# Four 32-byte gaps in the tile pools of an attention and two-layer kernel

## The chip, the core and the metric

The kernel runs on one core of one Trainium2 chip. The metric is the device time of one execution in microseconds (us). The kernel before was timed in three runs: 2345.20, 2345.23 and 2346.77 us, median 2345.23.

## What is computed

```python
def _attn_ref(q, k, v, tau):                     # q, k, v: 2 x 6016 x 256, float32
    qn = q / (np.linalg.norm(q, axis=1, keepdims=True) + 1e-06)
    kn = k / (np.linalg.norm(k, axis=1, keepdims=True) + 1e-06)
    s = kn.transpose(0, 2, 1) @ qn / tau
    a = np.exp(s - s.max(-1, keepdims=True))
    a /= a.sum(-1, keepdims=True) + 1e-09
    return v @ a
x = attn_out.reshape(12032, 256)
h = x @ w_in                                     # w_in: 256 x 2048
x = (h - np.tanh(h)) @ w_out                     # w_out: 2048 x 256
gate = 1.0 / (1.0 + np.exp(-(x @ w_gate)))       # w_gate, w_val: 256 x 1536
out = (gate * (x @ w_val)) @ w_out2              # w_out2: 1536 x 256
```

## The kernel before

The 12032 tokens are cut into 24 blocks, 12 for each batch. A block is 500 tokens wide in 20 of the 24; blocks 6 and 18 are 512 wide and blocks 7 and 19 are 504 wide. A first stage (about the first 100 us) loads q and k of batch 0 and forms their 256 x 256 product, its softmax and the product of that matrix with w_in, so that each batch has its own input weights (tiles awh and awl, the "hi" and "lo" halves of a float32 split in two float32r numbers). For batch 1 the same is done in between, beside the blocks of batch 0.

From then on a block p is four families of matmuls, all of them 128 x 128 weights against a moving operand as wide as the block:

- H (lines 324 and 326): the weights awh and awl against vTh and vTl, 16 groups of 6 matmuls a block.
- X (lines 370, 371 and 373): the weights w1h and w1l against the split activations g, 16 groups of 6.
- GV (lines 405, 406 and 408): the weights wgh, wgl, wvh and wvl against x2h and x2l, 12 groups of 12.
- O (line 437): the weights w2h and w2l against the split products p, 12 groups of 6.

Two blocks run interleaved: a slot of the main loop has one group of H of block p, one of GV of block p-1, one of X of block p (two groups behind its H) and one of O of block p-1, in this order on TensorE; some slots have no GV, no O or neither, so that a block has 408 matmuls, 192 of them H and X. X and O are built alike: four matmuls on the hi half with hi and lo weights, then two on the lo half with hi weights, moving operands from the same pool "rr". The first block, and the first four groups of block 1, do X in plain float32 (line 365). The main loop is written out under a manual schedule, so the order on every engine is the program's, with no planner.

The tiles lie in pools, one pool after another in the order in which they are opened, and in a pool tag after tag in the order of first use. A tile takes its bytes per partition, rounded up to 32. Every big tile here is a multiple of 64 bytes, so what a tile's start is modulo 64 comes from the small tiles ahead of it. The program of the kernel before has these starts, in bytes in the partition:

| tiles | used as | start | modulo 64 | modulo 128 |
|---|---|---|---|---|
| pool const: ones, ident, 4 tiles of 4 bytes (32 each) | | 16512 | 0 | 0 |
| pool wp: awh, awl, w1h, w1l (2048 each) | weights of H and X | 17664 | 0 | 0 |
| pools wk, cv, rr, sx (2048 each) | moving: g, p; float32 X | 83200 | 0 | 0 |
| pool one: x2h, x2l, vTh, vTl (4096 each) | moving of GV and H | 134400 | 0 | 0 |
| pool one: rn, mx, sm (32 each), then aT, acc (2048 each) | aT, acc: moving of GV of block 0, weights of line 285 | 150880 | 32 | 96 |
| pool wp2: wgh, wgl, wvh, wvl, w2h, w2l (2048 each) | weights of GV and O | 154976 | 32 | 96 |

wp2 takes the place of the pools boot1, boot4, boot6 and boot3 of the first stage, which are opened at the same 154976 and closed before it. In them raw (q and k) is both weights and moving operand of line 562.

All slices within these tiles begin at a multiple of 512 bytes, so a slice is where its tile is, modulo 64 and modulo 128.

TensorE loads the weights of the next matmul (rows "PEld") beside the running one, so at any time two reads of the partition run: the moving operand of matmul i and the weights of matmul i+1.

Of the kernel before, what the change touches and what calls it, by code (L numbers as in the profile page):

```python
# [8 lines left out]
F32 = mybir.dt.float32  # L9
# [8 lines left out]
P = 128  # L18
# [8 lines left out]
def kernel(  # L27
# [46 lines left out]
    const = ctx.enter_context(tc.tile_pool(name="const", bufs=1))  # L74
    wp = ctx.enter_context(tc.tile_pool(name="wp", bufs=1))
# [6 lines left out]
    one_p = ctx.enter_context(tc.tile_pool(name="one", bufs=1))  # L82
# [14 lines left out]
    def psw(name, shape=(P, 512)):  # L97
        return ps_w.tile(list(shape), F32, tag="w", name=name)
# [15 lines left out]
    aw_lo = {}  # L114
    w1_hi = [wp.tile([P, 2, C], F32R, name=f"w1h{i}") for i in range(N1 // 2)]
    w1_lo = {}
    win_d = dr_p.tile([N1 // 2, P, NK, 2 * P], F32, name="win_d")

    def conv(src, shape, pool, tag, name, w=None, hi=None, lo=None):
# [78 lines left out]
    def norm_mm(b, sq, sk, first, last):  # L198

        for o, xs in ((0, sq), (2, sk)):  # L200
            for i, x in enumerate(xs):
                for ct in range(2):
                    MM(nrm[b][:, o + ct, :], x[:, ct * P:(ct + 1) * P], ones[:, :NW],
                       start=first and o + i + ct == 0, stop=last and i == len(xs) - 1, skip_group_check=True)

    def s_softmax(b, sq, sk):

        np_ = nrm.get(b)
        if np_ is None:
            np_ = nrm[b] = psw(f"n{b}", (P, 4, NW))  # L210
        norm_mm(b, sq, sk, b == 1, True)
        yield
        rn = one_p.tile([P, 4], F32, tag="rn", name=f"rn{b}")
        nc.scalar.activation(rn, np_[:, :, 0], AF.Sqrt)
        if b == 0:
            nc.scalar.activation(dummy, dummy, AF.Exp)
        yield
        nc.vector.tensor_scalar_add(rn, rn, 1e-6)
        nc.vector.reciprocal(rn, rn)

        dg = (cv if b else wk)(f"dg{b}", (P, 2, P))
        for ct in range(2):
            nc.vector.tensor_scalar(dg[:, ct, :], ident, rn[:, ct:ct + 1], None, ALU.mult)
        nc.vector.tensor_scalar(rn[:, 2:4], rn[:, 2:4], rtau[:, 0:1], None, ALU.mult)
        s = (cv if b else wk)(f"s{b}", (P, 2, C))
        if b:
            yield
        for ct in range(2):
            nc.scalar.activation(
                s[:, ct, :], (ks[b] if b else kq[b])[:, ct, :], AF.Copy, scale=rn[:, 2 + ct:3 + ct]  # L230
            )
        if b:
            yield
        rq = psw(f"rq{b}", (P, 2, P))
        for ct in range(2):
            MM(rq[:, ct, :], ones, dg[:, ct, :], start=ct == 0, stop=True, skip_group_check=True)
        yield
        mx = one_p.tile([P, 2], F32, tag="mx", name=f"mx{b}")
        for ct in range(2):
            nc.vector.tensor_tensor(  # L240
                out=s[:, ct, :], in0=s[:, ct, :], in1=rq.rearrange("p a c -> p (a c)"), op=ALU.mult
            )
            nc.vector.tensor_reduce(
                out=mx[:, ct:ct + 1], in_=s[:, ct, :], axis=AX.X, op=ALU.max, negate=True
            )
        yield
        sm = one_p.tile([P, 2], F32, tag="sm", name=f"sm{b}")
        for ct in range(2):
            nc.scalar.activation(
                s[:, ct, :], s[:, ct, :], AF.Exp, bias=mx[:, ct:ct + 1], accum_out=sm[:, ct:ct + 1]  # L250
            )
        yield
        for ct in range(2):
            sc = sm[:, ct:ct + 1]
            nc.vector.tensor_scalar_add(sc, sc, 1e-9)
            nc.vector.reciprocal(sc, sc)
            nc.vector.tensor_scalar(s[:, ct, :], s[:, ct, :], sc, None, ALU.mult)
        if b:
            yield
        else:  # L260
            aT[b] = one_p.tile([P, 2, C], F32, tag="aT", name=f"aT{b}")
        ep = psw(f"ep{b}", (P, 2, C)) if b else None
        for ct in range(2):
            cs = slice(ct * P, (ct + 1) * P)
            e = ep[:, :, cs] if b else psw(f"ep{b}_{ct}", (P, 2, P))
            for kk in range(2):
                nc.tensor.transpose(e[:, kk, :], s[:, ct, kk * P:(kk + 1) * P], ident)
            if b == 0:
                nc.scalar.activation(aT[b][:, :, cs], e, AF.Copy)
        yield  # L270
        if b:
            hi = one_p.tile([P, 2, C], F32R, tag="aT", name=f"aTh{b}")
            lo = one_p.tile([P, 2, C], F32R, tag="acc", name=f"aTl{b}")
            nc.scalar.activation(hi, ep, AF.Copy)
            nc.vector.tensor_tensor(out=lo, in0=ep, in1=hi.bitcast(F32), op=ALU.subtract)
            aT[b] = (hi, lo)
# [246 lines left out]
    cb_t = const.tile([P, 1], F32, name="cb")  # L523
    ct_t = const.tile([P, 1], F32, name="ct")
    dummy = const.tile([P, 1], F32, name="dummy")
    nc.vector.memset(cb_t, CB)
    nc.vector.memset(ct_t, -HT * HT)
    cb, ct2 = cb_t[:, 0:1], ct_t[:, 0:1]
# [3 lines left out]
    with tc.tile_pool(name="boot1", bufs=1) as boot1, tc.tile_pool(name="boot4", bufs=4) as boot4, \  # L532
# [99 lines left out]


        sm0 = s_softmax(0, *sq)
        tv = split_v(0)
        for step in (tail[0], tail[0], tail[0], tv, tail[1], tv, sm0, sm0, e_mm, e_mm, sm0, tail[1], e_mm, e_mm,
# [6 lines left out]
        next(w6)  # L643

    wp2 = ctx.enter_context(tc.tile_pool(name="wp2", bufs=1))
    wg_hi, wg_lo, wv_hi, wv_lo = (
        [wp2.tile([P, 2, 2 * P], F32R, name=f"{nm}{i}") for i in range(N2 // 2)]
        for nm in ("wgh", "wgl", "wvh", "wvl")
# [69 lines left out]
    for j in range(NT):  # L718
        t = 54 + 2 * j
        at(t - 2, s1_load, j)  # L720
        at(t, s1_square, j)
    ts = t + 1
    at(ts, lambda: s_softmax(1, [acc[1][:, 0, :]], [acc[1][:, 1, :]]))
    at(20, e_out)
    at(28, e_out)
# [115 lines left out]
```

## Time and profile before

| | |
|---|---|
| time, median of three runs | 2345.23 us |
| span of the profiled execution, first to last instruction | 2342.6 us |
| TensorE (PE) busy | 2330.5 us, 99% of the span |
| weight loads (PEld) busy | 1932.8 us, 83% |
| VectorE (DVE) busy | 1799.2 us, 77% |
| ScalarE (ACT) busy | 1575.5 us, 67% |
| GpSimd (POOL) busy | 67.2 us, 3% |
| matmuls | 10338 |

The profiled execution has only its span; the median of the runs is 2.6 us above it, for what lies around the first and the last instruction. Matmuls overlap in the trace (a duration of 386 ns, while the next starts after some 224 ns), so what a matmul costs is read from the distance of two starts, or from a stretch of time divided by the matmuls in it, and not from its duration.

### The profile page before, as it was taken

The numbers are of one execution on the slowest core, as the hardware profiler recorded it, in microseconds if no ns is written. First come the engines' busy times: TensorE is split into PE (matmuls) and PEld (weight loads), VectorE is DVE, ScalarE is ACT, GpSimd is POOL, SyncE is SP. The second block draws the span as 40 slices with busy tenths as digits, with TensorE's granted clock in tenths as the row PEclk, the third lists the DMA queues.
The fourth block names the chain that finished last, engine by engine and source line by source line (L and its number), as shares of the span: only waits on it lengthen the run. The fifth ranks groups of instructions, "written<-read, shape, count | busy, mean of one in ns | idle before, by whom it ended". The sixth has DMA issues, their size and how long they took to land.

```text
span 2342.6 us, 28855 instructions
## 1 busy us (share of the span) xinstructions
PE 2330.5 (99%) x10338; PEld 1932.8 (83%) x10338; DVE 1799.2 (77%) x2791; ACT 1575.5 (67%) x2777; POOL 67.2 (3%) x53
## 2 busy tenths in 40 slices
PE   9999999999999999999999999999999999999999
PEld 7778788888888888888888888888888888888887
DVE  7999877787878777777777777777777777777773
ACT  6677666776767667766676666666666666666663
POOL 0000000111111110000000000000000000000000
PEclk9999999999999999999999999999999999999999
DMA  9742001101101100000000000000000000000000
GB/s 353 225 132 90 27 1 50 33 26 50 32 28 45 32 27 18 1 23 32 18 18 14 6 18 1 18 18 1 18 18 1 18 18 1 18 1 18 10 1 18
DMA packets 54000, 86.54 MB, mean 37 GB/s; under 512 B 4960, under 2 KB 34144, under 8 KB 53856
## 3 DMA queue, kind: packets, MB, share of 16 engines
q1 hardware_dynamic: 53280, 83.91, 11.1%
q8 instruction: 81, 1.33, 0.2%
q10 hardware_dynamic: 576, 0.79, 0.1%
q14 instruction: 63, 0.52, 0.1%
HBM read 69.73 MB, written 14.94 MB: 36 GB/s over the span
## 4 chain that ended last, share of the span: by engine, by line
PE 90%; DVE 7%; ACT 1%; issue 1%; DMA 0%; ACTq 0%; DVEq 0%; SPq 0%
PE o L437 16%; PE h L324 14%; PE h L326 7%; PE x L373 7%; PE x L370 7%; PE x L371 7%; PE ga L405 5%; PE ga L406 5%; PE va L405 5%; PE va L406 5%; PE ga L408 5%; PE va L408 5%; DVE accb L573 1%; DVE w L341 1%; DVE w L342 1%
## 5 line engine op out<-in xcount | busy, mean ns | idle before, releaser
L339 DVE SCALAR_TENSOR_TENSOR w<-u,h 128x500 f32<-128x500 f32 (+2 forms) x384 | 259.3, 675 | 327.0 <-ACT t L335 326.8
L334 ACT ACTIVATE u<-h 128x500 f32<-128x500 f32 (+2 forms) x384 | 223.7, 583 | 248.0 <-PE h L326 245.5
L342 DVE COPY_PREDICATED w<-m,t 128x500 f32<-128x500 uint16 (+2 forms) x384 | 306.2, 797 | 39.9 <-ACT sr L679 0.5
L337 ACT ACTIVATE s<-u,cb 128x500 f32<-128x500 f32 (+2 forms) x384 | 274.5, 715 | 0.7 <-DVE w L341 0.6
L338 ACT ACTIVATE m<-u,ct 128x500 bf16<-128x500 f32 (+2 forms) x384 | 272.8, 710 | 0.0
L340 DVE TENSOR_TENSOR t<-h,t 128x500 f32<-128x500 f32 (+2 forms) x384 | 258.2, 672 | 0.0
L341 DVE SCALAR_TENSOR_TENSOR w<-s,w 128x500 f32<-128x500 f32 (+2 forms) x384 | 257.3, 670 | 0.0
L324 PE MATMUL h<-vTh,awh 128*128 128x500 f32 (+2 forms) x768 | 243.9, 399 | 0.0
L324 PE MATMUL h<-vTl,awh 128*128 128x500 f32 (+2 forms) x768 | 235.4, 387 | 0.9 <-DVE vTl L311 0.9
L326 PE MATMUL h<-vTh,awl 128*128 128x500 f32 (+2 forms) x768 | 235.5, 388 | 0.0
L335 ACT ACTIVATE t<-h 128x500 f32<-128x500 f32 (+2 forms) x384 | 223.6, 582 | 1.7 <-PE x L365 1.0
L405 PE MATMUL ga<-x2h,wgh 128*128 128x500 f32 (+2 forms) x552 | 213.6, 387 | 0.0
L406 PE MATMUL va<-x2h,wvl 128*128 128x500 f32 (+2 forms) x552 | 213.6, 387 | 0.0
L406 PE MATMUL ga<-x2h,wgl 128*128 128x500 f32 (+2 forms) x552 | 213.6, 387 | 0.0
L405 PE MATMUL va<-x2h,wvh 128*128 128x500 f32 (+2 forms) x552 | 213.4, 387 | 0.0
L417 DVE TENSOR_TENSOR sg<-va,sg 128x500 f32<-128x500 f32 (+2 forms) x288 | 192.3, 668 | 20.9 <-PE va L408 20.9
L416 ACT ACTIVATE sg<-ga 128x500 f32<-128x500 f32 (+2 forms) x288 | 169.2, 587 | 15.7 <-PE ga L408 12.8
L408 PE MATMUL ga<-x2l,wgh 128*128 128x500 f32 (+2 forms) x576 | 176.1, 387 | 0.0
L408 PE MATMUL va<-x2l,wvh 128*128 128x500 f32 (+2 forms) x576 | 176.0, 387 | 0.0
L324 PEld LDWEIGHTS h<-vTh,awh 128*128 128x128 f32 x768 | 143.6, 188 | 34.5 <-issue 7.1
L324 PEld LDWEIGHTS h<-vTl,awh 128*128 128x128 f32 x768 | 144.4, 188 | 30.6 <-DVE vTl L311 1.4
L326 PEld LDWEIGHTS h<-vTh,awl 128*128 128x128 f32 x768 | 144.2, 188 | 28.9
(361 smaller groups left out, 4449.8 us busy)
## 6 DMA issues: line engine op xcount, KB each, us to landing
v<-in_v_dram SPq DMA_DIRECT2D x20, 500.0 KB, 4.2
out_dram<-ob SPq DMA_DIRECT2D x19, 500.0 KB, 3.2
sr<-in_q_dram SPq DMA_DIRECT2D x47, 128.0 KB, 2.1
sr<-in_k_dram SPq DMA_DIRECT2D x47, 128.0 KB, 2.2
raw<-in_q_dram SPq DMA_DIRECT2D x13, 384.0 KB, 8.1
raw<-in_k_dram SPq DMA_DIRECT2D x12, 384.0 KB, 8.2
st_wi<-in_moe_w_in_dram SPq DMA_DIRECT2D x8, 512.0 KB, 7.0
st_w<-in_moe_w_out_dram SPq DMA_DIRECT2D x8, 512.0 KB, 4.8
```

What stands on the lines that cost most here:

```text
L324: MM(o[:, :n], aw_hi[i][:, kk, fs], x[:, kk, :n], start=x is h and kk == 0, stop=False)
L326: MM(o[:, :n], aw_lo[i][:, kk, fs], h[:, kk, :n], start=False, stop=kk == 1)
L337: nc.scalar.activation(s, u, AF.Square, bias=cb)
L338: nc.scalar.activation(m, u, AF.Relu, bias=ct2)
L339: nc.vector.scalar_tensor_tensor(out=w, in0=u, scalar=C2, in1=hp, op0=ALU.mult, op1=ALU.mult)
L340: nc.vector.tensor_tensor(out=t, in0=hp, in1=t, op=ALU.subtract)
L341: nc.vector.scalar_tensor_tensor(out=w, in0=s, scalar=CG, in1=w, op0=ALU.add, op1=ALU.mult)
L342: nc.vector.copy_predicated(w, m.bitcast(U16), t)
L405: MM(o[:, :n], wht[m // 2][:, d, ms], h[d][:, :n], start=d == 0, stop=False)
L406: MM(o[:, :n], wlt[m // 2][:, d, ms], h[d][:, :n], start=False, stop=False)
L408: MM(o[:, :n], wht[m // 2][:, d, ms], lo[d][:, :n], start=False, stop=d == 1)
L437: MM(ops[p][d][:, :n], w[i][:, a, ds[d]], x, start=m == 0 and w is w2_hi and x is ph, stop=m == N2 - 1 and x is pl)
```

## The change

Four tiles of 8 float32 (32 bytes in the partition) are added that nothing writes or reads. One stands at the end of const, ahead of wp; one at the end of wp, ahead of wk; one in the pool one, between sm and aT; one at the start of wp2. No instruction is added or moved. Added up, const's gap moves wp by 32 bytes, with wp's gap everything from wk to vTl moves by 64, aT, acc and the pools of the first stage by 96, and the tiles of wp2 by 128.

```diff
@@ -114,6 +114,7 @@
     w1_hi = [wp.tile([P, 2, C], F32R, name=f"w1h{i}") for i in range(N1 // 2)]
     w1_lo = {}
+    wp.tile([P, 8], F32, name="half_row_w")
     win_d = dr_p.tile([N1 // 2, P, NK, 2 * P], F32, name="win_d")
@@ -258,6 +259,7 @@
         else:
+            one_p.tile([P, 8], F32, name="half_row_o")
             aT[b] = one_p.tile([P, 2, C], F32, tag="aT", name=f"aT{b}")
@@ -523,6 +525,7 @@
     dummy = const.tile([P, 1], F32, name="dummy")
+    const.tile([P, 8], F32, name="half_row")
     nc.vector.memset(cb_t, CB)
@@ -643,6 +646,7 @@
     wp2 = ctx.enter_context(tc.tile_pool(name="wp2", bufs=1))
+    wp2.tile([P, 8], F32, name="half_row_2")
     wg_hi, wg_lo, wv_hi, wv_lo = (
```

| tiles | start after, modulo 64 | modulo 128 |
|---|---|---|
| weights of H and X (wp) | 32 | 32 |
| weights of GV and O (wp2) | 32 | 96 |
| moving operands: wk, cv, rr, sx, x2h, x2l, vTh, vTl | 0 | 64 |
| aT, acc | 0 | 64 |
| pools of the first stage | 0 | 64 |

## Rows read from the trace of the kernel before

**Rows 1.** The page: busy time and share of the span; granted clock in 40 slices.

```profile
PE 2330.5 (99%) x10338; PEld 1932.8 (83%) x10338; DVE 1799.2 (77%) x2791; ACT 1575.5 (67%) x2777; POOL 67.2 (3%) x53
PEclk9999999999999999999999999999999999999999
```

**Rows 2.** Waits of PE, longest in total: us, times, longest.

```profile
PE kq L562 <- DMA raw<-in_k_dram: 2.5, 2, 1.4
PE va L406 <- DVE wvl L150: 1.3, 1, 1.3
```

**Rows 3.** Busy time by stretch of time: length, then each engine's us (instructions), PEclk.

```profile
core 0: us, PE busy (x) PEld busy (x) DVE busy (x) ACT busy (x) POOL busy (x), PEclk, DMA share, GB/s
...
260.00:620.00 360.00, 360.00 (x1600) 300.58 (x1599) 278.42 (x415) 248.09 (x445) 30.14 (x21) 1.00 0.10 31
620.00:720.00 100.00, 99.92 (x442) 82.60 (x441) 80.86 (x117) 71.47 (x129) 11.39 (x9) 1.00 0.11 32
720.00:830.00 110.00, 110.00 (x480) 89.95 (x479) 87.75 (x127) 77.85 (x140) 13.90 (x10) 1.00 0.14 44
...
920.00:1100.00 180.00, 180.00 (x806) 150.52 (x805) 138.09 (x227) 126.54 (x227) 0.00 (x0) 1.00 0.05 17
...
1200.00:1730.00 530.00, 530.00 (x2374) 445.60 (x2373) 397.62 (x622) 355.76 (x631) 0.00 (x0) 1.00 0.03 10
...
1935.00:2020.00 85.00, 85.00 (x378) 70.76 (x377) 62.72 (x98) 55.60 (x99) 0.00 (x0) 1.00 0.00 1
2020.00:2290.00 270.00, 270.00 (x1201) 225.44 (x1200) 197.94 (x310) 177.04 (x315) 0.00 (x0) 1.00 0.03 10
```

**Rows 4.** Timeline of PE, a slot near 500 us: start us, us, engine, line.

```profile
500.46 0.62 PE L324 MATMUL h<-vTh,awh 128*128 128x500 f32 x2
...
501.82 0.39 PE L405 MATMUL ga<-x2h,wgh 128*128 128x500 f32 x1
...
504.51 0.39 PE L370 MATMUL x<-g_11h,w1h 128*128 128x500 f32 x1
...
505.87 0.39 PE L437 MATMUL o<-p_7h,w2h 128*128 128x500 f32 x1
...
507.22 0.62 PE L324 MATMUL h<-vTh,awh 128*128 128x500 f32 x2
```

**Rows 5.** Timeline of PE, a slot near 1205 us.

```profile
1204.93 0.61 PE L324 MATMUL h<-vTh,awh 128*128 128x500 f32 x2
...
1206.27 0.39 PE L405 MATMUL ga<-x2h,wgh 128*128 128x500 f32 x1
...
1208.95 0.39 PE L370 MATMUL x<-g_3h,w1h 128*128 128x500 f32 x1
...
1210.29 0.39 PE L437 MATMUL o<-p_1h,w2h 128*128 128x500 f32 x1
...
1211.63 0.61 PE L324 MATMUL h<-vTh,awh 128*128 128x500 f32 x2
```

**Rows 6.** Timeline of PE, GV of block 0 and the X behind it.

```profile
210.54 0.39 PE L405 MATMUL ga<-x2aT,wgh 128*128 128x500 f32 x1
...
213.27 0.39 PE L370 MATMUL x<-g_10h,w1h 128*128 128x500 f32 x1
```

**Rows 7.** Timeline of PE, groups that are 512 wide: H, then O.

```profile
691.33 0.63 PE L324 MATMUL h<-vTh,awh 128*128 128x512 f32 x2
...
692.71 0.39 PE L370 MATMUL x<-g_12h,w1h 128*128 128x512 f32 x1
...
764.49 0.39 PE L437 MATMUL o<-p_5h,w2h 128*128 128x512 f32 x1
...
765.89 0.62 PE L324 MATMUL h<-vTh,awh 128*128 128x504 f32 x2
```

**Rows 8.** Groups by line and shape, PE: float32 matmuls; busy us, mean ns of one.

```profile
L509 PE MATMUL kqe<-er 128*128 128x256 f32 x160 | 38.6, 379 | 0.0
...
L285 PE MATMUL aw<-win,aT 128*128 128x256 f32 x64 | 15.1, 379 | 0.0
```

## The prediction

> **What bounds the kernel now.** First the page: PE is busy for 99% of the span and all 40 slices show the full granted clock, so every stretch below is at the 2.4 GHz level and no part of the difference is a clock that fell [rows 1]. Then the waits of PE: the longest cause comes to 2.5 us in all and lies in the first stage, the next to 1.3 us in block 0 [rows 2]. So from block 2 on nothing holds PE but PE, and DVE at 77% and ACT at 67% have room to follow if it gets faster. The time is the number of matmuls times the distance from one start to the next.
>
> That distance isn't the same everywhere, though the width is. By stretch [rows 3]: from 260 to 620 us there are 1600 matmuls in 360 us, 225.0 ns each; from 2020 to 2290 us 1201 in 270, 224.8 ns; but from 1200 to 1730 us 2374 in 530, 223.25 ns. All three hold blocks 500 wide and the same mix of families. One slot of each tells which family differs. Near 500 us [rows 4] the six matmuls of H take 501.82 - 500.46 = 1.36 us, 226.7 ns each; the twelve of GV 2.69, 224.2 ns; the six of X 1.36, 226.7 ns; the six of O 1.35, 225.0 ns. Near 1205 us [rows 5] H, X and O take 1.34 us, 223.3 ns each, and GV 2.68, 223.3 ns. So H and X have two speeds, and GV and O nearly one.
>
> X and O have the same order of six, the same width and the same pool of moving operands. They differ in their weights: those of X begin at 0 modulo 64, as the moving operand does, and those of O at 32. H is like X, GV like O. A third case lies in block 0, where the hi half that GV moves is in aT and acc, at 32, and the weights in wp2 are at 32 as well: equal again, and its twelve take 213.27 - 210.54 = 2.73 us, 227.5 ns, against 2.68 to 2.69 in later blocks with the same weights [rows 4 to 6]. So equal starts go with the slow distance in three families and two pools, unequal ones with the fast. The sizes fit reads in steps of that kind: 64 bytes of a float32 row pass in 16 / 2.4 = 6.67 ns, and 226.7 ns are 34.0 of these, 223.3 ns 33.5 (both estimates from rows 4 and 5). That H and X also run at 223.3 in one long stretch [rows 5] says that equal starts can fall into either pattern, as the stretch before leaves them.
>
> **The change, part by part.** It adds no instruction, wait or transfer; only addresses move. After it every matmul of the four families has moving operand at 0 and next weights at 32, the relation of GV and O.
>
> 1. Blocks 500 wide: I take the distance of the fast stretch, 223.25 ns, for all [rows 3]. Stretch 260 to 620: 1600 x (225.0 - 223.25) = 2.8 us. 2020 to 2290: 1201 x (224.8 - 223.25) = 1.9 us. 920 to 1100: its count holds the narrow matmuls of batch 1's softmax, so its own quotient can't be used; at the rate of the stretch from 2020, 180 us x 1.55 / 224.8 would be 1.2, and I take 1.1 since its first part still has 504-wide groups in it. Together 5.8 us. Bounds: nothing, if H and X keep their pattern; 7.3 us, if all go to 223.0, the lower edge of what 2.68 / 12 and 1.34 / 6 can mean at 0.01 us a start.
>
> 2. Stretches with 504-wide groups: 1935 to 2020 has 378 matmuls at 224.9 ns, of them 12 in 30 H and X. Between the two values of rows 4 and 5 these lie at some 225, so 151 x 1.8 ns = 0.3 us; the stretch from 830 to 920 is its twin (0.25). From 720 to 830 us and its twin, H and X are 504 wide beside 512-wide GV and O, at 229.2 ns in the mean; no row shows 504 with unequal starts alone. Bounds 0 and 0.7 us; I take 0.35, the middle. Together 0.9 us.
>
> 3. Blocks 512 wide speak against the change. Six of H with equal starts take 692.71 - 691.33 = 1.38 us, 230.0 ns; six of O with unequal ones 765.89 - 764.49 = 1.40, 233.3 ns [rows 7]. Two blocks of 192 H and X matmuls pay up to 384 x 3.3 ns = 1.3 us; the resolution lets it be 0.6. I take a loss of 1.0 us.
>
> 4. Blocks 0 and 1: GV of block 0 gets unequal starts, as aT and acc go to 0: twelve groups x 0.045 us = 0.5 us. The 500-wide H of both blocks would give 192 x 2.5 ns = 0.5, but PE also waits for others there, so half of it counts: 0.8 us together, bounds 0 and 1.2.
>
> 5. The float32 matmuls: line 509 has moving and weights both at 0, line 285 in batch 0 moving at 0 and weights at 32, and both have 379 ns [rows 8]. Price nothing. The first stage keeps equal starts in raw, now at 0; its DMAs land at 0 instead of 32. The row that could gain is the wait for raw, 2.5 us in all [rows 2]; I take nothing, bounds 0 and 1. That wp2 now lies 32 bytes further over the pools of the first stage adds neighbours to its tiles' wait for them, but those are older chunks of raw, and the first tiles are written after the stage's end. Writes of ACT and DVE into moved tiles aren't on PE's path.
>
> The sum: 5.8 + 0.9 - 1.0 + 0.8 = 6.5 us off a span of 2342.6 us, 2336.1 us; with the 2.6 us that the median has over it, 2338.7 us. Its own range by the bounds: gains of 7.3 + 1.2 + 1.2 + 1.0 less 0.6 at best, 2335.1 us; at worst nothing in the 504-wide and first blocks, 1.3 us lost in the wide ones and a point 1 that reaches 5, 2341.5 us.
>
> **The rivals.** No effect: the two reads don't meet, and X is slower than O for another reason, such as its place in the slot or its pool. Then the time is 2345.2, give or take 1 us. For it: the same addresses run at 223.3 for 500 us [rows 5], so equal starts alone don't make it slow. Against it: GV of block 0, which slows with its moving operand's start while place and weights stay [rows 6]. The Trainium skill ("TensorE: Matmul & The Clock Gate", section "Step-by-step: what each phase is for") states that TensorE reads weights and moving operand by two independent ports, so that loading the next weights takes nothing from the running matmul; by that rule the time would be this rival's, 2345.2 us. That X and O, alike in shape, differ by 3 ns near 500 us doesn't fit the rule read strictly, but no row moves one address alone.
>
> The other side: what counts is the distance modulo 128. So far GV and O have 96 and are fast, and equal starts have 0; after the change H and X have 96, but GV and O have 32, since their moving operands move by 64 and wp2 by 128. If 32 is a bad distance like 0, the 20 blocks 500 wide pay 216 x 20 x 3.4 ns = 14.7 us in GV and O, against 6.5 us won: 2353 us. It ends above 2345 as soon as GV and O lose over 1.5 ns each. Against it: half of 64 bytes, 0.5 x 6.67 ns, is already the step between the patterns.
>
> Only half: with one relation throughout, H stays at 34 steps through something in its order (it alternates two halves of vTh at each matmul). Then half of points 1 and 2 is left, 2345.2 - 3 = 2342 us.
>
> **How the numbers follow.** Forecast 0.62, no effect 0.24, the 128-byte distance 0.08, only half 0.06. About 0.2%, 4.7 us, is what a measurement can tell from no change. Faster by more means below 2340.5: most of the forecast's range, 0.60. Within 0.2%: its upper edge, no effect and half, 0.32. Slower: 0.08. The range for 8 in 10 runs from 2335.0, the lower bound of the sum, to 2346.0, which takes in no effect. The likeliest case alone is 2335.1 to 2341.5.
>
> **What would show it.** In the same stretches the quotient should be near 223.25 ns in all three (some 1612 matmuls from 260 to 620 us), H and X slots 1.34 us near 500 us, GV of block 0 2.68, H of block 6 about 1.40. H and X still at 1.36 and GV unmoved is no effect; GV and O at 1.36 and 2.72 is the 128-byte distance. A span that shrinks with these distances unchanged would make the reason wrong.

## The result: slower by 1.1%

| | before | after |
|---|---|---|
| time, median (lowest to highest of 4) | 2345.22 us (2344.97 to 2346.77) | 2370.79 us (2370.55 to 2371.03) |
| ratio, 95% interval | 1 | 1.0107, 1.0093 to 1.0121 |
| span of the profiled execution | 2342.6 us | 2368.7 us |

The forecast of 2338.7 us was wrong, and the time lies far above its range (2335.0 to 2346.0). The page of the kernel after answers to [rows 1]: PE is busy for the whole span, with the full granted clock in all slices, and DVE and ACT do the same work as before.

```profile
PE 2357.2 (100%) x10338; PEld 1932.5 (82%) x10338; DVE 1799.7 (76%) x2791; ACT 1576.0 (67%) x2777; POOL 67.2 (3%) x53
PEclk9999999999999999999999999999999999999999
```

Nor does PE wait more than in [rows 2]; the wait for raw even fell from 2.5 to 1.9 us:

```profile
PE kq L565 <- DMA raw<-in_k_dram: 1.9, 2, 1.2
PE va L408 <- DVE wvl L151: 1.3, 1, 1.3
```

So the 26.1 us that the span grew by (the median by 25.6) are again a matter of the distance from one matmul's start to the next. Busy time by stretch, to be held against [rows 3]:

```profile
core 0: us, PE busy (x) PEld busy (x) DVE busy (x) ACT busy (x) POOL busy (x), PEclk, DMA share, GB/s
...
260.00:620.00 360.00, 360.00 (x1584) 297.41 (x1583) 275.25 (x411) 245.61 (x440) 29.30 (x21) 1.00 0.10 31
...
1200.00:1730.00 530.00, 530.00 (x2333) 437.91 (x2332) 390.14 (x611) 351.72 (x624) 0.00 (x0) 1.00 0.04 12
...
2020.00:2290.00 270.00, 270.00 (x1189) 223.06 (x1188) 200.36 (x314) 179.58 (x319) 0.00 (x0) 1.00 0.03 10
```

Divided, these are 227.3, 227.2 and 227.1 ns, where before had 225.0, 223.25 and 224.8. The distances did become the same in all stretches, as forecast, but at a slow value. A slot of the timeline, beside [rows 5] (the lines are two further down the file than before):

```profile
1208.27 0.61 PE L326 MATMUL h<-vTh,awh 128*128 128x500 f32 x2
...
1209.63 0.39 PE L407 MATMUL ga<-x2h,wgh 128*128 128x500 f32 x1
...
1212.37 0.39 PE L372 MATMUL x<-g_2h,w1h 128*128 128x500 f32 x1
...
1213.74 0.39 PE L439 MATMUL o<-p_0h,w2h 128*128 128x500 f32 x1
...
1215.11 0.61 PE L326 MATMUL h<-vTh,awh 128*128 128x500 f32 x2
```

H takes 1.36 us, GV 2.74, X 1.37, O 1.37; before 1.34, 2.68, 1.34, 1.34. Summed over the trace, from start to start and by family and width, after less before:

| family | 500 wide | 504 wide | 512 wide |
|---|---|---|---|
| H | +2.5 us (442.7 to 445.2) | +0.2 | +0.7 |
| X | +2.2 us (408.7 to 410.9) | -0.6 | +0.5 |
| GV | +12.3 us (645.7 to 658.0) | +0.9 | -0.2 |
| O | +6.7 us (322.6 to 329.3) | +0.5 | +0.2 |

Together 25.8 of the 26.1 us, and 19.0 of them in GV and O 500 wide, which were to stay as they were.

**A correction to what stands ahead of the prediction.** By the order of first use the gap of wp lies between w1h and w1l, not behind both. After the change awh, awl and w1h begin at 32 modulo 64, but w1l at 66880, which is 0 modulo 64. A third of X's matmuls (line 373 of the kernel after) thus doesn't have what the change's words and the table say. The tables also stop at modulo 128. Modulo 256, which turned out to matter, the starts are:

| | before | after |
|---|---|---|
| moving operands of H, X, GV, O | 0 | 64 |
| awh, awl, w1h / w1l | 0 / 0 | 32 / 64 |
| wp2 (weights of GV and O) | 96 | 224 |
| aT, acc | 96 | 192 |
| **weights less moving: H and X** | 0 | 224 (w1l: 0) |
| **weights less moving: GV and O** | 96 | 160 |

### The profile page after: what moved, and what is told of

Read it like the earlier page. It is cut to its first block, busy times and chain, and to the rows that moved or that the text cites. A ratio compares the mean times of both kernels' runs of the same rounds, so it can differ in the third digit from the quotient of the medians.

```text
span 2368.7 us, 28855 instructions
## 1 busy us (share of the span) xinstructions
PE 2357.2 (100%) x10338; PEld 1932.5 (82%) x10338; DVE 1799.7 (76%) x2791; ACT 1576.0 (67%) x2777; POOL 67.2 (3%) x53
## 4 chain that ended last, share of the span: by engine, by line
PE 92%; DVE 5%; DMA 2%; issue 1%; ACT 1%; ACTq 0%; SPq 0%; DVEq 0%
PE o L439 16%; PE h L326 14%; PE h L328 7%; PE x L375 7%; PE x L373 7%; PE x L372 7%; PE ga L408 5%; PE va L408 5%; PE ga L407 5%; PE va L407 5%; PE ga L410 5%; PE va L410 5%; DVE w L343 1%; DVE w L341 0%; DVE w L344 0%
## 5 line engine op out<-in xcount | busy, mean ns | idle before, releaser
L336 ACT ACTIVATE u<-h 128x500 f32<-128x500 f32 (+2 forms) x384 | 223.7, 582 | 269.5 <-PE h L328 269.0
L337 ACT ACTIVATE t<-h 128x500 f32<-128x500 f32 (+2 forms) x384 | 223.7, 582 | 1.7 <-PE x L367 1.0
L407 PE MATMUL va<-x2h,wvh 128*128 128x500 f32 (+2 forms) x552 | 215.8, 391 | 0.0
L407 PE MATMUL ga<-x2h,wgh 128*128 128x500 f32 (+2 forms) x552 | 215.8, 391 | 0.0
L408 PE MATMUL va<-x2h,wvl 128*128 128x500 f32 (+2 forms) x552 | 215.8, 391 | 0.0
```

The lines of the kernel that those rows point to most:

```text
L407: MM(o[:, :n], wht[m // 2][:, d, ms], h[d][:, :n], start=d == 0, stop=False)
L408: MM(o[:, :n], wlt[m // 2][:, d, ms], h[d][:, :n], start=False, stop=False)
```

## The experiments

In all of them only gaps are set, of so many bytes in the partition: G1 ahead of the pool wp (moves everything from wp on), G2 ahead of wk (moves the moving operands and what follows), G4 at the start of wp2 (weights of GV and O alone), G0 ahead of const (moves everything). None of them has the gaps of the change. With n bytes they are (G0 is a pool of its own like G1, ahead of const):

```diff
+    ctx.enter_context(tc.tile_pool(name="gap_1", bufs=1)).tile([P, n // 4], F32, name="gap_1_t")
     wp = ctx.enter_context(tc.tile_pool(name="wp", bufs=1))
+    ctx.enter_context(tc.tile_pool(name="gap_2", bufs=1)).tile([P, n // 4], F32, name="gap_2_t")
     wk_p = ctx.enter_context(tc.tile_pool(name="wk", bufs=6))
...
     wp2 = ctx.enter_context(tc.tile_pool(name="wp2", bufs=1))
+    wp2.tile([P, n // 4], F32, name="gap_4")
```

D below is the start of a family's weights less the start of its moving operand, modulo 256. "Distance" in ns is start to start of matmuls 500 wide. The distances are means over the trace's matmuls, without the few over 300 ns where PE waited. Ratios are against the kernel before on the same chip, whose medians there are 2345.0 to 2345.3 us. The theories, by the letters that some expectations use: M, the moving operand's own start modulo 128 counts (64 is bad); R, the distance modulo 128 counts; D, the distance modulo 256 counts; L, the place of the weights counts; B, every distance from 32 to 128 is good; S, 96 is best and what is near it nearly as good.

### Does a start count, or a distance modulo 128?

**mv64**: G2 = 64, G4 = 64. The moving operands go to 64, the weights of H and X stay. D is 192 for H and X, 160 for GV and O.

> Only the moving operands are moved: a gap of 64 bytes ahead of the pool wk and one of 64 ahead of the tiles of wp2, so that x2h, x2l, vTh, vTl, g and p begin at 64 modulo 128 (before: 0), while the weights keep their starts modulo 128 (0 for H and X, 96 for GV and O). Theory M (what counts is the moving operand's own start, 0 or 64 modulo 128): all four families go to the distances of the changed kernel, 227 to 229 ns, time near 2371 us. Theory R (what counts is the distance from the moving operand to the next weights modulo 128): GV and O, at 32 as in the changed kernel, go to some 228 ns; H and X are at 64, not seen so far. At least 2365 us if H and X stay at 226.7. If neither counts, 2345 us.

Measured: 2374.63 us, ratio 1.0125 (1.0108 to 1.0141). H and X have 228.9 ns, GV and O 226.67. Slow in all four families, with no gap at the weights of H and X at all.

```profile
1200.00:1730.00 530.00, 530.00 (x2336) 438.91 (x2335) 390.67 (x612) 350.25 (x622) 0.00 (x0) 1.00 0.04 12
```

**all64**: G0 = 64. Everything moves by 64, D is as before.

> Every tile is moved by 64 bytes, by one gap ahead of the pool const; all distances between tiles are as before. Theory M (the moving operand's own start modulo 128): GV and O at some 228 ns, H and X at 226.7 or more, time 2365 to 2375 us. Theory R (the distance to the weights): everything as before, H and X between 223.5 and 226.7, GV and O at 223.5, time 2345 us, give or take 3.

Measured: 2345.33 us, 1.0001 (0.9991 to 1.001), and by stretch the counts of [rows 3] to one matmul:

```profile
260.00:620.00 360.00, 360.00 (x1601) 300.57 (x1600) 278.44 (x416) 248.48 (x445) 30.11 (x21) 1.00 0.10 31
...
1200.00:1730.00 530.00, 530.00 (x2375) 445.67 (x2374) 397.68 (x622) 355.86 (x632) 0.00 (x0) 1.00 0.03 10
```

The moving operands stand where the change puts them, at 64, and nothing is lost. M falls: a shift of everything by 64 bytes changes nothing, so differences count. (No shift by 32 was run.)

**w32**: G1 = 32, G2 = 96. D is 160 for H and X, 96 for GV and O as before.

> Only the weights of H and X are moved, all of them, to 32 modulo 128, by a gap of 32 bytes ahead of wp and one of 96 ahead of wk; moving operands and wp2 keep their starts modulo 128 (0 and 96). Theory M: GV and O stay at 223.5 ns; H and X have a moving operand at 0 and weights at another start, so they go to 223.3 or stay at 225.4; time 2338 to 2346 us. Theory R: H and X are at the distance 32 that GV and O have in the changed kernel, so they go to some 228 ns: 3800 x 2.5 ns = 10 us more, 2355 us.

Measured: 2356.19 us, 1.0046 (1.0031 to 1.0061). H and X 226.55 ns throughout, where before had 223.5 in this long stretch; GV 224.0, O 224.6.

```profile
1200.00:1730.00 530.00, 530.00 (x2354) 441.78 (x2353) 393.51 (x615) 352.88 (x627) 0.00 (x0) 1.00 0.04 12
```

**w96**: G1 = 96, G2 = 32. D is 224 for H and X, which is 96 modulo 128, the relation of GV and O.

> Only the weights of H and X are moved, to 96 modulo 128, by a gap of 96 bytes ahead of wp and one of 32 ahead of wk; moving operands (0) and wp2 (96) keep theirs. Every matmul of the four families then has the starts that GV and O had before. Theory R and the sum of the prediction: H and X at 223.3 ns, 2338 to 2340 us. Theory M, with weights that don't count: 2345 us. If a uniform relation all through falls in another pattern, GV and O leave 223.5 too.

Measured: 2357.02 us, 1.0051 (1.0036 to 1.0066). H and X 229.1 ns, GV 223.2, O 223.06.

```profile
1200.00:1730.00 530.00, 530.00 (x2347) 441.08 (x2346) 391.52 (x614) 351.09 (x624) 0.00 (x0) 1.00 0.04 12
```

H and X at 96 modulo 128 are slow beside GV and O, which are fast at 96 modulo 128. So R falls too: the two relations are alike modulo 128 (and 64), and differ by 128 bytes.

### Modulo 256

**d96_512**: G1 = 96, G2 = 416. The weights of H and X lie at the addresses of w96; the moving operands are moved further, and D is 96 in all families, modulo 512 as well.

> Distance here is the start of the next matmul's weights less the start of the running matmul's moving operand, modulo 256. Before: 0 for H and X, 96 for GV and O. A gap of 96 bytes ahead of wp and of 416 ahead of wk puts all four families at 96, modulo 512 too. Theory D (this distance decides, and 96 is the fast one): H and X at 223.3 ns, time 2338 us or less. Theory L (the place of the weights decides: H and X slow at any distance but 0, since their weights lie in wp): H and X at 226.5 to 229 as with 224 and 160, time 2354 to 2358 us.

Measured: 2339.41 us, 0.9976 (0.9967 to 0.9985). All four families have 223.33 ns in all stretches. (The quotients, 360 / 1614 = 223.05, 530 / 2375 = 223.16 and 270 / 1210 = 223.14, lie a little lower, since a stretch also counts the matmuls that its ends cut.)

```profile
260.00:620.00 360.00, 360.00 (x1614) 302.73 (x1612) 280.70 (x420) 250.19 (x449) 30.07 (x21) 1.00 0.10 31
...
1200.00:1730.00 530.00, 530.00 (x2375) 445.75 (x2374) 397.06 (x621) 355.63 (x630) 0.00 (x0) 1.00 0.03 10
...
2020.00:2290.00 270.00, 270.00 (x1210) 227.12 (x1209) 197.73 (x310) 177.01 (x315) 0.00 (x0) 1.00 0.02 8
```

From w96 to here the weights of H and X don't move, and their matmuls go from 229.1 to 223.33 ns. L falls.

**d96_256**: G1 = 96, G2 = 160. As d96_512, but D of H and X is 352 modulo 512.

> As the one before, but the second gap is 160 bytes, so that H and X are at 96 modulo 256 and 352 modulo 512, GV and O at 96 modulo both less nothing moved. Theory D with a period of 256: the same time as with 416, 2338 us. With a period of 512 or more: H and X elsewhere, 226 to 229 ns, 2350 us or more. Theory L: 2354 to 2358 us.

Measured: 2339.88 us, 0.9977 (0.9968 to 0.9987), 223.33 ns in all families. 256 bytes more between weights and moving operand make no difference, 128 do (w96): the period is 256, as far as the distance 96 shows it; no other was run with 256 bytes more.

```profile
260.00:620.00 360.00, 360.00 (x1614) 302.75 (x1613) 280.59 (x420) 249.34 (x447) 30.08 (x21) 1.00 0.10 31
```

**go160**: G4 = 64 alone. The weights of GV and O get the D that the change gives them, 160; H and X keep 0.

> One part alone, the weights of GV and O: a gap of 64 bytes at the start of wp2, which puts them at distance 160 as in the changed kernel; H and X stay at 0. Theory D: GV and O go from 223.5 to between 226.7 (as with moving operands alone moved) and 228.2 (changed kernel), 5000 x 3.2 to 4.7 ns = 16 to 23 us more, 2361 to 2368 us. Theory L, where wp2 is a good place: 2345 us.

Measured: 2368.28 us, 1.0099 (1.0082 to 1.0115). One gap costs 23.3 us against the kernel before of its own runs, and the change costs 25.6. By the same sums as for the kernel after, 18.2 us of this lie in GV and O 500 wide, which lose 19.0 in the change, but 4.3 lie in H and X 500 wide, whose own distance is still 0: in the stretch of [rows 5] they have 225.8 ns, after 223.5. GV and O have two patterns at 160, 226.67 ns in that stretch and 228.7 in the others. The timeline of a slot beside [rows 4], now in the order X, O, H, GV, X: GV takes 509.05 - 506.31 = 2.74 us (2.69 before), O 1.37 (1.35), X and H 1.36 as before.

```profile
502.22 0.39 PE L370 MATMUL x<-g_10h,w1h 128*128 128x500 f32 x1
...
503.58 0.39 PE L437 MATMUL o<-p_6h,w2h 128*128 128x500 f32 x1
...
504.95 0.62 PE L324 MATMUL h<-vTh,awh 128*128 128x500 f32 x2
...
506.31 0.39 PE L405 MATMUL ga<-x2h,wgh 128*128 128x500 f32 x1
...
509.05 0.39 PE L370 MATMUL x<-g_11h,w1h 128*128 128x500 f32 x1
```

**hx224**: G1 = 32, G2 = 32. H and X get the change's D, 224; GV and O keep 96. Other addresses than w96, the same distances.

> The changed kernel's other part: the gap of 32 ahead of wp and one of 32 ahead of wk, so that moving operands move by 64 as in the changed kernel and H and X are at 224 (w1l too), while wp2 moves with the moving operands and GV and O stay at 96. Theory D: GV and O at 223.2 to 223.5, H and X at 229 as in the kernel with weights at 96 modulo 128, 2355 to 2358 us. If moving the moving operand costs by itself, GV and O stay at 227 to 228 and the time is near 2371 us.

Measured: 2356.96 us, 1.0051 (1.0036 to 1.0066), and the distances of w96: H and X 229.1 ns, GV 223.2. In the slot H takes 1.38 us, GV 2.67, X 1.38, O 1.34:

```profile
502.01 0.63 PE L326 MATMUL h<-vTh,awh 128*128 128x500 f32 x2
...
503.39 0.39 PE L407 MATMUL ga<-x2h,wgh 128*128 128x500 f32 x1
...
506.06 0.39 PE L372 MATMUL x<-g_11h,w1h 128*128 128x500 f32 x1
...
507.44 0.39 PE L439 MATMUL o<-p_7h,w2h 128*128 128x500 f32 x1
...
508.78 0.63 PE L326 MATMUL h<-vTh,awh 128*128 128x500 f32 x2
```

The parts don't add up: go160 loses 23.3 us and hx224 11.9, together 35.2, the change 25.6. H and X at 224 have 229.1 ns beside families at 96, but 226.67 beside families at 160. A family's pattern depends on its neighbours too.

### One distance for all families

In these the four families have the same D, so that neighbours can't mix in: G1 = D, G2 = 256 - D, and G4 = D - 96 modulo 256 (zero gaps left out).

**u0**: G4 = 160.

> All four families at distance 0 (modulo 256), as H and X were before; a gap of 160 bytes at the start of wp2. It tells which of the two patterns of distance 0 holds when nothing disturbs it. At 226.7 ns all through: some 10000 x 1.8 ns = 18 us over the kernel before with an opposite 1.5 from stretches already slow, 2358 us. At 223.5 all through: 2338 to 2340 us. Theory D says only that all four families have one value.

Measured: 2343.02 us, 0.9991 (0.9981 to 1.0). Two patterns in one run, neither of the two cases expected: 226.67 ns early, 223.33 later.

```profile
260.00:620.00 360.00, 360.00 (x1590) 298.77 (x1589) 276.42 (x413) 246.49 (x442) 30.12 (x21) 1.00 0.10 31
...
1200.00:1730.00 530.00, 530.00 (x2375) 445.49 (x2374) 397.70 (x622) 355.93 (x632) 0.00 (x0) 1.00 0.03 11
```

**u32**: G1 = 32, G2 = 224, G4 = 192.

> All four families at distance 32. Theory B (only weights at or shortly behind the moving operand's place, modulo 256, meet it, so every distance from 32 to 128 is free): 223.3 ns, 2339 us. Theory S (the distance gets better step by step up to 96 and worse behind it): between 0 and 96, 224 to 226 ns, 2342 to 2358 us.

Measured: 2374.82 us, 1.0123 (1.0108 to 1.0138), 228.0 ns. B falls.

```profile
260.00:620.00 360.00, 360.00 (x1580) 296.65 (x1580) 274.43 (x410) 245.00 (x439) 28.34 (x20) 1.00 0.10 31
```

**u64**: G1 = 64, G2 = 192, G4 = 224.

> All four families at distance 64. Theory B: 223.3 ns, 2339 us. Theory S: 223.5 to 225 ns, 2340 to 2352 us. If it beats the kernel with all at 96, a smaller modulus hides another effect.

Measured: 2315.42 us (2314.98 to 2316.76), 0.9873 (0.9858 to 0.9887): 220.00 ns in all families and stretches, faster than both kernels. S falls. By stretch 1637, 2408 and 1229 matmuls, where [rows 3] have 1600, 2374 and 1201; in the slot H takes 1.32 us, GV 2.64, X 1.32:

```profile
260.00:620.00 360.00, 360.00 (x1637) 306.91 (x1636) 285.83 (x427) 254.66 (x457) 31.04 (x22) 1.00 0.10 31
...
1200.00:1730.00 530.00, 530.00 (x2408) 451.77 (x2407) 405.63 (x634) 362.20 (x646) 0.00 (x0) 1.00 0.04 12
...
2020.00:2290.00 270.00, 270.00 (x1229) 230.39 (x1228) 191.52 (x300) 171.78 (x306) 0.00 (x0) 1.00 0.02 8
```

```profile
506.02 0.60 PE L326 MATMUL h<-vTh,awh 128*128 128x500 f32 x2
...
507.34 0.38 PE L407 MATMUL ga<-x2h,wgh 128*128 128x500 f32 x1
...
509.98 0.38 PE L372 MATMUL x<-g_13h,w1h 128*128 128x500 f32 x1
...
511.30 0.60 PE L326 MATMUL h<-vTh,awh 128*128 128x500 f32 x2
```

**u128**: G1 = 128, G2 = 128, G4 = 32.

> All four families at distance 128. Theory B: 223.3 ns, 2339 us. Theory S, with 96 the best and 160 at 226.7 to 228.7: 224.5 to 226 ns, 2348 to 2362 us.

Measured: 2367.80 us, 1.0095 (1.008 to 1.011), 226.67 ns in this stretch as in the others.

```profile
260.00:620.00 360.00, 360.00 (x1590) 298.08 (x1589) 276.21 (x413) 246.19 (x441) 29.89 (x21) 1.00 0.10 31
```

### The changed kernel's own distances, the last one, and the width

**u160**: G1 = 160, G2 = 96, G4 = 64; the change's D of GV and O for all.

> All four families at distance 160, where the changed kernel has GV and O. Slow by itself: one value between 226.7 and 228.7 ns for the 500-wide blocks, 2362 to 2378 us. Slow by alternation with H and X at another distance: 223 to 225 ns, below 2352 us. The steps seen so far (220.0 at 64, 223.3 at 96, 226.7 at 128) would go on to 230.0 ns, 2383 us.

Measured: 2378.83 us, 1.0144 (1.0129 to 1.0159), 228.9 ns (226.67 for the 500-wide stretch from 967 to 1113 us). The slowest of all: the D that the change gives GV and O is slow by itself, and it is slow with H and X at 0 (go160), 160 (here), 192 (mv64) and 224 (the change), at 226.67 to 228.9 ns.

```profile
260.00:620.00 360.00, 360.00 (x1575) 295.53 (x1574) 273.11 (x408) 243.69 (x436) 28.44 (x20) 1.00 0.10 31
```

**u224**: G1 = 224, G2 = 32, G4 = 128; the change's D of H and X for all.

> All four families at distance 224, where the changed kernel has H and two thirds of X. Slow by itself: 229 ns as in the kernels with H and X alone there, 2380 us. By alternation: 226.6 ns or less, below 2365 us.

Measured: 2365.00 us, 1.0088 (1.0071 to 1.0105), 226.67 ns, the distance that H has after the change. The 229.1 ns of w96 and hx224 don't come back: they belong to 224 beside families at 96.

```profile
260.00:620.00 360.00, 360.00 (x1590) 298.42 (x1589) 276.30 (x412) 246.36 (x442) 30.11 (x21) 1.00 0.10 31
```

**u192**: G1 = 192, G2 = 64, G4 = 96.

> All four families at distance 192. H and X alone at it had 228.9 ns beside GV and O at 160: by itself 228 to 230 ns, 2372 to 2384 us.

Measured: 2342.04 us (2341.39 to 2347.77), 0.9993 (0.9983 to 1.0002), 30 us below what was expected. Three patterns in one run: 228.9 ns, then 220.0, then 226.67, each for a whole stretch:

```profile
260.00:620.00 360.00, 360.00 (x1575) 297.78 (x1574) 273.15 (x408) 243.99 (x438) 28.37 (x20) 1.00 0.11 31
...
1200.00:1730.00 530.00, 530.00 (x2411) 452.29 (x2410) 404.25 (x631) 358.65 (x641) 0.00 (x0) 1.00 0.04 11
...
2020.00:2290.00 270.00, 270.00 (x1193) 223.64 (x1192) 194.66 (x305) 174.34 (x311) 0.00 (x0) 1.00 0.02 6
```

The trace shows where the first change of pattern lies. H takes 1.37 us ahead of four 128-wide matmuls of batch 1's softmax, and 1.32 us behind them:

```profile
959.79 0.62 PE L326 MATMUL h<-vTh,awh 128*128 128x500 f32 x2
...
961.16 0.39 PE L407 MATMUL ga<-x2h,wgh 128*128 128x500 f32 x1
...
965.28 0.60 PE L269 MATMUL ep<-ident,s 128*128 128x128 f32 x4
...
972.33 0.60 PE L326 MATMUL h<-vTh,awh 128*128 128x500 f32 x2
...
973.65 0.38 PE L407 MATMUL ga<-x2h,wgh 128*128 128x500 f32 x1
```

**u64_502**: the gaps of u64, and the tokens cut into 8 blocks of 502 and 4 of 500 for each batch, in place of 500, 504 and 512:

```diff
-        x = min(rest, TB - WB)
+        x = min(rest, 2)
```

> All four families at distance 64, and the 16 spare tokens of a batch go by twos to 8 blocks of 502 instead of one of 512 and one of 504. If the price at 64 is a step that 502 shares with 500 (220.0 ns): the blocks of 512 and 504 lose their 228 to 233 ns, 816 x (13 + 8.4) ns = 17 us less than with 512 and 504, 2298 us. If 502 falls on the next half step (223.3 ns): 16 blocks x 408 x 3.3 ns = 22 us back, 2320 us.

Measured: 2339.20 us, 0.9975 (0.9966 to 0.9985), above both cases expected. The matmuls 500 wide have 220.0 to 220.7 ns, those 502 wide 226.67 beside each other: two columns more cost 6.67 ns, and most of u64's gain goes.

```profile
1200.00:1730.00 530.00, 530.00 (x2379) 446.48 (x2378) 398.39 (x622) 355.21 (x631) 0.00 (x0) 1.00 0.03 10
...
2020.00:2290.00 270.00, 270.00 (x1193) 223.68 (x1192) 195.56 (x305) 174.64 (x310) 0.00 (x0) 1.00 0.02 7
```

## Why the prediction was wrong

**The step that failed** is one sentence: "After it every matmul of the four families has moving operand at 0 and next weights at 32, the relation of GV and O." It took the relation modulo 64. The rows of before hold two relations, equal and 96 apart (and GV of block 0, equal), and so can't tell a period of 64 from 128 or 256; the forecast chose the first without a row that bears it. By the period that the runs show, the change carries GV and O from 96 to 160 and H and X from 0 to 224, and neither of the new relations occurs in the trace of before. The 500-wide matmuls of GV, from 96 to 160, went from 223.7 to 228.0 ns in the mean, those of O from 223.6 to 228.3.

- Point 1, 500 wide: forecast 5.8 us won, by H and X. They lost 4.8, because they have some 226.6 ns throughout and no longer fall into 223.5 in the stretch of [rows 5]. How much of that is their own 224 isn't told apart: in go160 they keep 0 and lose 4.3 beside GV and O at 160. GV and O, priced at nothing, lost 19.0. That 160 is slow is shown by u160, and that moving GV and O there alone makes most of the loss by go160.
- The price of the relation was right: where all four families do have a distance of 96 modulo 256, the time is 2339.4 and 2339.9 us (d96_512, d96_256), beside a sum of 2338.7. By parts, the 500-wide matmuls of d96_256 win 6.8 us, where points 1 and 4 had 6.6, the 504-wide ones 0.3 in place of 0.9, and the 512-wide ones lose 1.4 in place of 1.0.
- Point 2, 504 wide: 0.9 us won forecast, 1.0 lost (0.2 - 0.6 + 0.9 + 0.5), by the same step.
- Point 3, 512 wide: 1.0 us lost forecast for H and X, 1.1 measured, but by luck: they have 233.4 and 232.4 ns at 224, where 233.3 was priced for 96.
- Point 4: GV of block 0 was to win 0.5 us; it takes 213.80 - 211.08 = 2.72 us, after 2.73 in [rows 6]. The distance of its hi half went from 0 to 32 modulo 256, and u32 shows 32 to be no better; that of its lo half (in sx) went from 96 to 160.
- Point 5: the float32 matmuls of line 285 went from a distance of 96 to 160 and take 215.6 ns start to start, after 215.8; no price, as said. The wait for raw gave 0.6 us, within its bounds.
- What bounds the kernel was read rightly: PE is busy for 99 to 100% of the span in every run, the time follows the distances of its matmuls, and no wait took their place.
- Two slips carry nothing: by [rows 4] X and O differ by 1.7 ns near 500 us, not 3; and the worst end of the sum's range takes 5 us for point 1, though its own bound is nothing.

**The rivals.** The 128-byte distance had the right family and the right side, and the sign that it named, GV at 2.72 us and more, is in the trace. Its period was wrong (w96) and its size too small: it took 3.4 ns for each matmul of GV and O, where the change cost 4.3 in GV and 4.6 in O (12.3 us over 2880 matmuls, 6.7 over 1439), and it gave H and X a gain. The argument that held it at 0.08, that the patterns differ by half of 6.67 ns, is about time and says nothing on the period in addresses. The rival "no effect" falls: matmuls of one shape took 220.0 to 228.9 ns here with nothing changed but where their operands start, 2315.4 to 2378.8 us in all. The Trainium skill ("TensorE: Matmul & The Clock Gate", section "Step-by-step: what each phase is for") states that loading the next weights takes no read bandwidth from the running matmul. These runs don't bear that out as a rule for the time from start to start, and the measurement decides. The rival "only half" falls too: H has 223.33 ns in d96_512 with its order unchanged.

**What stays open.** At 0, 160 and 192 one program runs in several patterns, a stretch each, so the distance doesn't set the time by itself. From 260 us on, no trace shows a change of pattern while all matmuls are 500 wide; the changes lie where others pass between: at 965 us in u192 (128 wide, above), behind some 1100 us in the kernel before, u0, u160 and go160 (256 wide), and behind the 512- and 504-wide blocks. This fits the prediction's word that the stretch before leaves the pattern; why one follows from another, and whether the width or what else happens there decides, wasn't found. Nor was why H and X at 224 have 229.1 ns beside families at 96 and 226.67 otherwise. All weights of a family start alike modulo 256 in the experiments, so the runs can't say whether the weights of the running or of the next matmul are what counts; that the next one's load overlaps with the running matmul makes the latter likely, but this is argued. Which part of the memory the two reads share was not shown either, nor that other engines' reads and writes have no part in it; their work takes the same time in all runs (DVE 1798 to 1801 us busy, ACT 1571 to 1577), and so do the weight loads (PEld 1931 to 1938).

## What to carry over

Where PE is bound by float32r matmuls with a weight load for each, the start of the weights less the start of the moving operand, modulo 256, moves the distance between matmuls, here by up to 4%: of the eight multiples of 32, try them all, for the width in use and for all families together, since the best is not the same for 500, 504 and 512 columns and a family's time depends on its neighbours. Here the gaps of u64 are worth 1.3%. Read the starts from the program as built, since a gap tile lies where its first use puts it. And a relation found in a trace holds for the residues that the trace contains: before a change carries operands to new ones, ask which longer periods the same rows would fit.

## What the runs showed of the hardware that was not expected

Distance start to start by D in ns, four families alike (u0 to u224, and d96_256 for 96). For 500 wide these are the values of stretches of that width alone; for 504 and 512 wide, which always stand beside groups of another width, the lowest and highest of the four families' means:

| D modulo 256 | 500 wide | 504 wide | 512 wide |
|---|---|---|---|
| 0 | 226.67 or 223.33 | 226.8 to 227.0 | 226.8 to 230.4 |
| 32 | 228.0 | 229.8 to 229.9 | 232.6 to 233.3 |
| 64 | 220.00 | 228.1 to 229.0 | 232.6 to 233.2 |
| 96 | 223.33 | 226.7 to 227.8 | 232.9 to 233.8 |
| 128 | 226.67 | 230.6 to 233.3 | 231.4 to 233.1 |
| 160 | 228.9 or 226.67 | 227.1 to 228.9 | 233.2 to 233.6 |
| 192 | 228.9, 220.0 or 226.67 | 229.2 to 229.5 | 228.4 to 228.9 |
| 224 | 226.67 | 227.0 to 227.6 | 233.1 to 233.5 |

The values 220.0, 223.33 and 226.67 are 33, 33.5 and 34 times 6.67 ns, the time of 16 columns at 2.4 GHz (an estimate from these rows); 228.0 and 228.9 fit no half step, at 34.2 and 34.3 of them. The change from 500 to 502 columns at 64 is one whole step, though it adds only two columns. So the time of a matmul isn't proportional to its width here, and 500 columns at 64 are cheaper for each column (0.440 ns) than the 512 of H and X at 0 (226.9 ns, 0.443).
